# A Fourier mixing layer and two expert layers on one core: conversion steps, first tiles and one weight load in another order

## The chip, the cores and the metric

The kernel runs on one core of a Trainium2 chip, all in 32-bit floats. The time is the device time of one execution in microseconds (us). The engines are TensorE (PE, with its weight loads as PEld), VectorE (DVE), ScalarE (ACT), GpSimd (POOL) and SyncE (SP), which here issues nearly all transfers. Each engine runs its own instructions strictly in the order in which the program gives them; they meet through semaphores.

## The reference

```python
def _attn_ref(x, w_r, w_i, b_r, b_i):            # x: 2 x 3008 x 256
    X = np.fft.rfft(x, axis=1)
    Xr, Xi = (X.real.astype(np.float32), X.imag.astype(np.float32))
    Yr = Xr @ w_r - Xi @ w_i + b_r
    Yi = Xr @ w_i + Xi @ w_r + b_i
    lam = 0.01
    Yr = np.sign(Yr) * np.maximum(np.abs(Yr) - lam, 0.0)
    Yi = np.sign(Yi) * np.maximum(np.abs(Yi) - lam, 0.0)
    Y = Yr.astype(np.float64) + 1j * Yi.astype(np.float64)
    return np.fft.irfft(Y, n=x.shape[1], axis=1).astype(np.float32)

def _moe_ref(x, w_in, w_out):                    # 6016 x 256, hidden 2048
    h = x @ w_in
    return (h * np.clip(h + 3.0, 0.0, 6.0) / 6.0) @ w_out

def _moe2_ref(x, w_gate, w_val, w_out):          # hidden 1536
    g = x @ w_gate
    return (g * (1.0 / (1.0 + np.exp(-g))) * (x @ w_val)) @ w_out
```

The three run one after the other; the weights of the two expert layers come as 64-bit floats.

## The kernel before

The Fourier transform over 3008 = 47 x 64 points is done in two stages of small matrices. Stage one of batch 0 takes x in 16 tiles (`halves1(i)`): 8 matmuls of all 128 rows and 64 columns, two side by side in the array, and one copy into `zm`, by ScalarE for even tiles and VectorE for odd. Stage one of batch 1 takes 8 double tiles T0 to T7 (`quarters1(i)`): 32 matmuls of 64 rows and 64 columns, four side by side, into two PSUM banks, each copied by one engine, first 64 columns to `ze`, then the rest to `zm`.

Stage two goes by 12 quads p = 0 to 11 (6 of each batch): S(p) (`s2`) multiplies 8 blocks of `zm` or, for the first quad of batch 1, of `ze`, with a table `m`; ScalarE and VectorE evict it as X in a high and a low part, then in the same way the sum (`evict`, whose last part runs one work item later). ln(p,0) and ln(p,1) multiply X with the linear weights `linh`, `linl` (three matrices: real, imaginary and mixed sums), after a first matmul that puts the bias tile `shift` into PSUM; then k, yb, yc and yp take the threshold. A(p) (`ia`) is the first stage back, from yp of both halves and a table `n`; its result goes to DRAM. `post` does the second stage back for a pair of token blocks into `xa`.

All matmuls with weights run in three passes of a high and a low part. The expert weights come as 64-bit words in pieces of 256 a row and are put together by `Convert`: a call of `conv1.step()` moves a pipeline by one piece, with a load on SP (piece i+3), two operations of ScalarE (lines 174, 195) and four of VectorE (lines 199, 179, 192, 183). 32 pieces take 38 steps; the first three only load.

A unit (`unit()`) is one of 32 parts of the first expert layer on the first two token blocks: it makes its conversion steps, splits the previous unit's result (`lower`), projects with six matmuls into `ph`, gates, and accumulates the unit before the previous one with six matmuls into `acc`. Units n = 0 to 16 run inside the quads from p = 8 on, the rest in a loop behind.

The order is written by hand in the list `seq` of work items, one list for all engines; what an item leaves for later (`later`, `due`) is put behind the next item. `amid` holds the steps that prepare the linear weights and the bias; `halves1(i)` takes them out after its copy. The lines behind it:

```python
        if 0 < ORDER.index((b, Q)) < FROM:        # in ln; FROM = 8
            conv1.step()
```

```python
        for _ in range(2 - n % 2):                # in unit
            if not conv1.done():
                conv1.step()
```

PSUM has 8 banks, which the items take in turn until p = 7; from there the items take five in turn and `acc` has three. Behind all this, 903 of the 1133 us are the quads of the two expert layers, in which nothing is changed.

Of the kernel before, what the change touches and what calls it, by code (L numbers as in the profile page):

```python
# [81 lines left out]
def fourier_moe_kernel(ctx: ExitStack, tc: tile.TileContext, x, lin, bias, w1, w2, fwd1, inv2, fwd2,  # L82
# [176 lines left out]
    def prepare():  # L259
        lin_st = ring4("lin_st").rearrange("p (k a b) -> p k a b", k=2, a=2)  # L260
        b_st = spread("b_st")
        load_x(0, 1, every=some)
        nc.sync.dma_start(lin_st, lin)
        load_x(0, 2, every=some)
        for c in (slice(0, 2 * TC), slice(2 * TC, RC)):
# [21 lines left out]
        def shifts(i):  # L287
# [7 lines left out]
        amid.update({  # L295
            7: [lambda: mixed(ALU.subtract)], 8: [lambda: hi(2, 0)], 9: [lambda: mixed(ALU.add)],
            10: [lambda: hi(0, 2), lambda: lo(2, 0)], 11: [lambda: hi(1, 3)], 12: [lambda: lo(0, 2)],
            13: [lambda: lo(1, 3)], 14: [lambda: shifts(0)], 15: [lambda: shifts(1)]})

# [8 lines left out]
    def z(b, Q):  # L308
        return zm[:, Q - b] if Q >= b else ze

    def halves1(i):
        src = room[0, i // 4][:, i % 4 * TC : (i % 4 + 1) * TC]
        p = psf[0]([128, 512], f"p1_{i}")
        for n in range(ND):
            for c in range(2):
                at = 128 * n + 64 * c
                nc.tensor.matmul(p[64 * c : 64 * c + 64, n : n + ND * (2 * GC - 1) + 1 : ND], src[:, at : at + 64],
                                 fwd1_sb[:, : 2 * GC], start=True, stop=True, tile_position=(0, 64 * c))
        copy = (nc.scalar.copy, nc.vector.tensor_copy)[i % 2]
        to = zm.rearrange("p q g (r d) -> p (q g) r d", r=2)[:, :, :, ND * i : ND * (i + 1)]  # L320
        copy(to, p[:, : 2 * ND * GC].rearrange("p (a r n) -> p a r n", r=2, n=ND))
        for g in amid.pop(i, ()):
            g()

    def quarters1(i):
        src = room[1, i // 2][:, i % 2 * 2 * TC : (i % 2 + 1) * 2 * TC]
        p = [psf[0]([128, 512], f"p1_{i}_{r}") for r in range(2)]
        N = 2 * ND
# [6 lines left out]
        for r, copy in enumerate((nc.scalar.copy, nc.vector.tensor_copy)):  # L335
            c = slice(64 * r + N * i, 64 * r + N * (i + 1))
            q = p[r][:, : N * GC].rearrange("p (a n) -> p a n", n=N)
            copy(ze[:, :, c], q[:, :8])
            copy(zm[:, : NQ - 1, :, c].rearrange("p q g n -> p (q g) n"), q[:, 8:])

# [54 lines left out]
    def ln(b, Q, h):  # L395

        if (b, Q) not in n_t:
            n_t[b, Q] = table("n", inv1, Q, 4, f"n{b}_{Q}")
        if 0 < ORDER.index((b, Q)) < FROM:
            conv1.step()  # L400
# [63 lines left out]

    T = [[lambda i=i: quarters1(i)] for i in range(NT // 2)]

# [7 lines left out]

    seq = [prepare] + [lambda i=i: halves1(i) for i in range(NT)] + S(0) + [lambda: load_next(0)] + S(1)
    seq += [lambda: load_next(1)]
    for p in range(len(ORDER)):
        l, a, s = L(p), A(p - 1), S(p + 1) if p else []
        u = [lambda: unit()] if p >= FROM else []
        if p == FROM:  # L480
            seq += l[:1] + s + a + [lambda: post(0, 0), lambda: post(0, 1)] + u + l[1:] + u + u + u
        elif p == NQ + 1:
            seq += l[:1] + s + [lambda: load_first()] + a + l[1:]
        elif p == NQ - 3:
            seq += l[:1] + s + T[0] + a + T[1] + l[1:] + T[2]
        elif p == NQ - 2:
            seq += l[:1] + T[3] + s + T[4] + a + T[5] + l[1:] + T[6]
        elif p == NQ - 1:
            seq += l[:1] + T[7] + a + s + l[1:]
        else:  # L490
            seq += l[:1] + u + s + a + u + l[1:] + u + u
# [133 lines left out]
    def unit():  # L625
# [3 lines left out]

        for _ in range(2 - n % 2):  # L630
            if not conv1.done():
                conv1.step()
        if 0 <= n - 1 < len(units):
# [590 lines left out]
```

## Time and profile before

| what | value |
|---|---|
| median of 3 runs | 1134.98 us (1133.74 to 1135.16) |
| the profiled execution, time | 1134.5 us |
| the profiled execution, span | 1132.7 us |
| TensorE busy | 1117.3 us, 99% of the span |
| VectorE busy | 910.4 us, 80% |
| ScalarE busy | 776.8 us, 69% |
| granted clock of TensorE over the span | 0.999 |

The span runs from the first to the last instruction; 1.8 us of the execution lie around it. In a timeline row stand start and duration in us, engine, line, operation, the tile written and those read, the shape, a count where rows are merged, and in brackets the engine's idle time before and what ended it. A row of windows by stage holds the stretch, its length, the busy time of TensorE, its weight loads, VectorE, ScalarE and GpSimd with instruction counts, then the granted clock of TensorE (1.00 is 2.4 GHz, 0.50 is 1.2), the busy share of the transfers and GB/s. Matmuls overlap: the time of a block is the distance of two starts, and a wait is longer than its idle time shows by the part that the previous matmul covers.

### The profile page before, as it was taken

How to read it: one execution, taken by the hardware profiler on the slowest of the kernel's cores; microseconds unless marked ns; L12 is line 12 of the kernel's file. 1: busy time of each engine (PE TensorE's matmuls, PEld its weight loads, DVE VectorE, ACT ScalarE, POOL GpSimd, SP SyncE). 2: the span in 40 equal slices, each digit the busy share in tenths (PEclk: the TensorE clock that was granted, in tenths of full speed). 3: DMA queues.
4: the chain of work that ended last, by engine and by line, in shares of the span. 5: the costliest groups of instructions: out<-in, count | busy, mean ns of one | idle time of the engine just before them, and what ended most of it. 6: DMA issues, size and time to landing. Idle time of an engine off the chain costs nothing.

```text
span 1132.7 us, 19794 instructions
## 1 busy us (share of the span) xinstructions
PE 1117.3 (99%) x7468; PEld 989.2 (87%) x7468; DVE 910.4 (80%) x1635; ACT 776.8 (69%) x1440; POOL 41.4 (4%) x68
## 2 busy tenths in 40 slices
PE   8999999999999999999999999999999999999998
PEld 7988788888888888888899888888888888888997
DVE  5778996899999999999988777777777777777665
ACT  4667775688788788787787666666666666656655
POOL 2000004500000000000000000000000000000000
PEclk9999999999999999999999999999999999999999
DMA  7856434964473664554643544644644644644552
GB/s 288 275 168 191 147 108 144 316 226 171 136 253 109 197 225 154 182 199 149 211 175 127 195 167 167 242 167 168 241 167 168 241 167 168 237 168 168 207 207 75
DMA packets 62944, 211.49 MB, mean 187 GB/s; under 512 B 5984, under 2 KB 23552, under 8 KB 51392
## 3 DMA queue, kind: packets, MB, share of 16 engines
q1 hardware_dynamic: 60784, 203.61, 51.9%
q0 software_dynamic: 1776, 6.42, 1.4%
q8 instruction: 59, 0.97, 0.3%
q14 instruction: 37, 0.30, 0.1%
q10 hardware_dynamic: 288, 0.19, 0.1%
HBM read 170.09 MB, written 40.11 MB: 186 GB/s over the span
## 4 chain that ended last, share of the span: by engine, by line
PE 91%; DVE 5%; DMA 1%; ACT 1%; issue 1%; SPq 0%; ACTq 0%; DVEq 0%
PE acc L133 12%; PE acc L131 12%; PE acc L132 12%; PE P L912 8%; PE P L914 8%; PE P L913 8%; PE Tb L912 4%; PE Tb L913 4%; PE Tb L914 4%; PE Q L912 2%; PE Q L913 2%; PE Q L914 2%; PE p L440 2%; PE p L360 2%; PE p L551 1%
## 5 line engine op out<-in xcount | busy, mean ns | idle before, releaser
L969 ACT COPY hold<-P 128x512 f32<-128x512 f32 (+1 forms) x224 | 128.3, 573 | 57.9 <-PE P L914 56.4
L591 ACT CAST gated<-r 128x512 fp32r<-128x512 f32 (+1 forms) x160 | 98.1, 613 | 64.9 <-DVE r L960 63.3
L136 DVE TENSOR_TENSOR gated<-s,gated 128x512 fp32r<-128x512 f32 (+1 forms) x144 | 97.4, 676 | 49.8 <-ACT gated L1096 49.5
L136 DVE TENSOR_TENSOR gated<-r,gated 128x512 fp32r<-128x512 f32 (+1 forms) x160 | 107.8, 674 | 21.6 <-ACT gated L591 16.9
L131 PE MATMUL acc<-gated,w_o 128*128 128x512 f32 (+1 forms) x320 | 120.4, 376 | 0.0
L132 PE MATMUL acc<-gated,w_o 128*128 128x512 f32 (+1 forms) x320 | 119.6, 374 | 0.0
L133 PE MATMUL acc<-gated,w_o 128*128 128x512 f32 (+1 forms) x320 | 119.6, 374 | 0.0
L964 DVE TENSOR_TENSOR hold<-Q,hold 128x512 f32<-128x512 f32 (+1 forms) x112 | 75.7, 676 | 44.1 <-ACT hold L969 41.8
L133 PE MATMUL acc<-gated,slot 128*128 128x512 f32 (+1 forms) x288 | 108.1, 375 | 0.0
L131 PE MATMUL acc<-gated,slot 128*128 128x512 f32 (+1 forms) x288 | 108.0, 375 | 0.1
L132 PE MATMUL acc<-gated,slot 128*128 128x512 f32 (+1 forms) x288 | 107.9, 375 | 0.0
L964 DVE TENSOR_TENSOR hold<-P,hold 128x512 f32<-128x512 f32 (+1 forms) x112 | 75.7, 676 | 33.9 <-PE P L914 33.9
L1136 ACT ACTIVATE s<-hold 128x512 f32<-128x512 f32 (+1 forms) x72 | 44.9, 623 | 81.0 <-DVE hold L964 81.0
L956 ACT ACTIVATE r<-hold,consts 128x512 f32<-128x512 f32 (+1 forms) x120 | 85.5, 712 | 14.5 <-DVE hold L964 12.4
L912 PE MATMUL P<-xo,slot 128*128 128x512 f32 (+1 forms) x240 | 90.0, 375 | 1.5 <-DVE hold L964 1.4
L1096 ACT CAST gated<-s 128x512 fp32r<-128x512 f32 (+1 forms) x144 | 87.7, 609 | 3.5 <-DVE s L1151 3.3
L913 PE MATMUL P<-xo,slot 128*128 128x512 f32 (+1 forms) x240 | 88.8, 370 | 0.0
L914 PE MATMUL P<-xo,slot 128*128 128x512 f32 (+1 forms) x240 | 88.8, 370 | 0.0
L964 DVE TENSOR_TENSOR hold<-Tb,hold 128x512 f32<-128x512 f32 (+1 forms) x112 | 75.8, 676 | 14.2 <-PE Tb L914 10.5
L960 DVE SCALAR_TENSOR_TENSOR r<-r,hold 128x512 f32<-128x512 f32 (+1 forms) x120 | 80.8, 673 | 2.5 <-ACT r L956 1.4
L1141 ACT ACTIVATE s<-hold 128x512 f32<-128x512 f32 (+1 forms) x72 | 44.8, 622 | 45.7 <-DVE hold L964 45.7
L969 ACT COPY hold<-Tb 128x512 f32<-128x512 f32 (+1 forms) x112 | 65.0, 580 | 4.3 <-ACT hold L969 0.3
(189 smaller groups left out, 2835.0 us busy)
## 6 DMA issues: line engine op xcount, KB each, us to landing
slot<-Wd SPq DMA_DIRECT2D x72, 1152.0 KB
slot<-Sd SPq DMA_DIRECT2D x40, 896.0 KB
st<-in_w SPq DMA_DIRECT2D x68, 256.0 KB
Wd<-slot SPq DMA_DIRECT2D x12, 1152.0 KB
m<-in_fwd SPq DMA_DIRECT2D x12, 512.0 KB
Cd<-cs POOLq DMA_DIRECT2D x12, 512.0 KB, 5.8
Xd<-x SPq DMA_DIRECT2D x20, 256.0 KB
raw<-Xd SPq DMA_DIRECT2D x5, 1024.0 KB
```

The costliest lines, as they stand in the source:

```text
L131: nc.tensor.matmul(o, wl, xh, start=start, stop=False)
L132: nc.tensor.matmul(o, wh, xh, start=False, stop=False)
L133: nc.tensor.matmul(o, wh, xl, start=False, stop=stop)
L136: nc.vector.tensor_tensor(out=o, in0=full, in1=hi.bitcast(F32), op=ALU.subtract)
L591: nc.scalar.copy(hi[:, :n], g[:, :n])
L912: nc.tensor.matmul(o, wl, hi, start=start, stop=False, skip_group_check=not start)
L913: nc.tensor.matmul(o, wh, lo, start=False, stop=False, skip_group_check=not start)
L914: nc.tensor.matmul(o, wh, hi, start=False, stop=True, skip_group_check=not start)
L956: nc.scalar.activation(r[:, :n], x[:, :n], AF.Relu, bias=three)
L964: nc.vector.tensor_tensor(out=h, in0=x[:, :n], in1=c, op=ALU.add)
L969: nc.scalar.copy(c, x[:, :n])
L1096: nc.scalar.copy(hi[:, :nb], t[:, :nb])
```

## The change

Five things are put elsewhere; no arithmetic is changed.

- The linear weights are loaded behind the third of four slices of x, instead of ahead of it.
- Tiles 12 to 15 of batch 0 are made as two double tiles by `quarters1(0, 6)` and `quarters1(0, 7)`, which write only `zm`.
- The steps in `amid` are spread otherwise: four of them (high and low part of the second mixed weight, the two steps of the bias) now run after S(0) and its eviction, ahead of S(1).
- Conversion steps: quad 0 gets two, the double tiles 1, 2, 4, 5, 6, 7 of batch 1 one each, and each unit makes one instead of two and one by turns. The double tiles stand otherwise around A(3), S(5), A(4) and S(6).
- At p = 8, ln(8,1) stands directly behind the two `post` items, and one unit is taken out there; it runs in the loop behind.

```diff
         load_x(0, 1, every=some)
+        load_x(0, 2, every=some)
         nc.sync.dma_start(lin_st, lin)
-        load_x(0, 2, every=some)
...
         amid.update({
-            7: [lambda: mixed(ALU.subtract)], 8: [lambda: hi(2, 0)], 9: [lambda: mixed(ALU.add)],
...
+            14: [lambda: hi(1, 3), lambda: lo(1, 3), lambda: shifts(0), lambda: shifts(1)]})
...
+    def aside(i):
+        for g in amid.pop(i, ()):
+            g()
...
         for r, copy in enumerate((nc.scalar.copy, nc.vector.tensor_copy)):
...
-            copy(ze[:, :, c], q[:, :8])
-            copy(zm[:, : NQ - 1, :, c].rearrange("p q g n -> p (q g) n"), q[:, 8:])
+            if b:
+                copy(ze[:, :, c], q[:, :8])
+            copy(zm[:, : NQ - b, :, c].rearrange("p q g n -> p (q g) n"), q[:, 8 * b :])
+        if b and i not in (0, 3):
+            conv1.step()
+        if not b:
+            aside(NT // 2 - 2 + i)
...
-        if 0 < ORDER.index((b, Q)) < FROM:
+        if ORDER.index((b, Q)) < FROM:
             conv1.step()
...
-    seq = [prepare] + [lambda i=i: halves1(i) for i in range(NT)] + S(0) + [lambda: load_next(0)] + S(1)
+    seq = [prepare] + [lambda i=i: halves1(i) for i in range(NT - 4)]
+    seq += [lambda i=i: quarters1(0, i) for i in (6, 7)] + S(0) + [lambda: load_next(0), lambda: aside(14)] + S(1)
...
         if p == FROM:
-            seq += l[:1] + s + a + [lambda: post(0, 0), lambda: post(0, 1)] + u + l[1:] + u + u + u
+            seq += l[:1] + s + a + [lambda: post(0, 0), lambda: post(0, 1)] + l[1:] + u + u + u
...
         elif p == NQ - 2:
-            seq += l[:1] + T[3] + s + T[4] + a + T[5] + l[1:] + T[6]
+            seq += l[:1] + T[3] + a + T[4] + s + l[1:] + T[5]
         elif p == NQ - 1:
-            seq += l[:1] + T[7] + a + s + l[1:]
+            seq += l[:1] + T[6] + a + T[7] + s + l[1:]
...
-        for _ in range(2 - n % 2):
-            if not conv1.done():
-                conv1.step()
+        if not conv1.done():
+            conv1.step()
```

VectorE around S(0), before: `sum` and `X` with p_0_0 are the eviction of S(0), `linl` and `shift` the last steps of `amid`.

```order
L136 TENSOR_TENSOR linl<-mixed,linh 128x512
L290 TENSOR_SCALAR b_st<-b_st 64x512
L321 COPY zm<-p_15_316 128x96x4
L136 TENSOR_TENSOR shift<-b_st,shift 32x512
L372 TENSOR_TENSOR sum_0_0_348<-p_0_0_0_330,sum_0_0_348 128x256
L136 TENSOR_TENSOR X_0_329<-p_0_0_0_330,X_0_329 128x512
L372 TENSOR_TENSOR sum_0_1_353<-p_0_0_1_331,sum_0_1_353 128x256
```

The same place in the changed program, from the copy of the last double tile to the first of S(1)'s eviction:

```order
L343 COPY zm<-p_0_7_1_318 128x48x8
L136 TENSOR_TENSOR linl<-mixed,linh 128x512
L380 TENSOR_TENSOR sum_0_0_375<-p_0_0_0_357,sum_0_0_375 128x256
L136 TENSOR_TENSOR X_0_356<-p_0_0_0_357,X_0_356 128x512
L380 TENSOR_TENSOR sum_0_1_380<-p_0_0_1_358,sum_0_1_380 128x256
L136 TENSOR_TENSOR X_0_356<-p_0_0_1_358,X_0_356 128x512
L136 TENSOR_TENSOR X_0_356<-sum_0_0_375,X_0_356 128x256
L136 TENSOR_TENSOR X_0_356<-sum_0_1_380,X_0_356 128x256
L136 TENSOR_TENSOR linl<-mixed,linh 128x512
L290 TENSOR_SCALAR b_st<-b_st 64x512
L136 TENSOR_TENSOR shift<-b_st,shift 32x512
L380 TENSOR_TENSOR sum_1_0_417<-p_0_1_0_399,sum_1_0_417 128x256
```

The write of `shift` moved from ahead of S(0)'s eviction to behind the whole of it.

VectorE at the last double tile of batch 1, before: `ze` and `zm` with p_7_1 are T7's copies, `sum` with p_1_0 is S(6).

```order
L423 TENSOR_TENSOR yb_5_0_1255<-p_0_5_0_1232,k_5_0_1253 128x512
L338 COPY ze<-p_7_1_1260 128x8x8
L339 COPY zm<-p_7_1_1260 128x40x8
L429 SCALAR_TENSOR_TENSOR yp_5_0_1258<-yb_5_0_1255,yc_5_0_1257 128x512
L372 TENSOR_TENSOR sum_0_0_1334<-p_1_0_0_1316,sum_0_0_1334 128x256
```

And in the changed program, where the lines 199, 179, 192 and 183 are one conversion step:

```order
L431 TENSOR_TENSOR yb_5_0_1309<-p_0_5_0_1286,k_5_0_1307 128x512
L342 COPY ze<-p_1_6_1_1314 128x8x8
L343 COPY zm<-p_1_6_1_1314 128x40x8
L199 TENSOR_TENSOR w_o<-wt,w_o 128x256
L179 TENSOR_SCALAR wt<-head 128x256
L192 SCALAR_TENSOR_TENSOR wt<-head,wt 128x256
L183 SCALAR_TENSOR_TENSOR wt<-st,wt 128x256
L437 SCALAR_TENSOR_TENSOR yp_5_0_1312<-yb_5_0_1309,yc_5_0_1311 128x512
L342 COPY ze<-p_1_7_1_1379 128x8x8
L343 COPY zm<-p_1_7_1_1379 128x40x8
L199 TENSOR_TENSOR w_g<-wt,w_g 128x256
```

T7's copies moved behind T6's copies, a conversion step and yp, with the eviction of S(6) next but for one more step.

VectorE behind `post`, before: `xa` is the last low part of `post`, `r` with `ph` the gate of the first unit, `yb` that of ln(8,1).

```order
L136 TENSOR_TENSOR xa<-p_0_1_1_1784,xa 128x512
L199 TENSOR_TENSOR w_c<-wt,w_c 128x256
L179 TENSOR_SCALAR wt<-head 128x256
L192 SCALAR_TENSOR_TENSOR wt<-head,wt 128x256
L183 SCALAR_TENSOR_TENSOR wt<-st,wt 128x256
L199 TENSOR_TENSOR w_o<-wt,w_o 128x256
L179 TENSOR_SCALAR wt<-head 128x256
L192 SCALAR_TENSOR_TENSOR wt<-head,wt 128x256
L183 SCALAR_TENSOR_TENSOR wt<-st,wt 128x256
L576 SCALAR_TENSOR_TENSOR r<-r,ph 128x512
L423 TENSOR_TENSOR yb_2_1_1887<-p_1_2_1_1864,k_2_1_1885 128x512
```

And in the changed program:

```order
L136 TENSOR_TENSOR xa<-p_0_1_1_1897,xa 128x512
L431 TENSOR_TENSOR yb_2_1_1969<-p_1_2_1_1946,k_2_1_1967 128x512
L199 TENSOR_TENSOR w_g<-wt,w_g 128x256
L179 TENSOR_SCALAR wt<-head 128x256
L192 SCALAR_TENSOR_TENSOR wt<-head,wt 128x256
L183 SCALAR_TENSOR_TENSOR wt<-st,wt 128x256
L437 SCALAR_TENSOR_TENSOR yp_2_1_1972<-yb_2_1_1969,yc_2_1_1971 128x512
L585 SCALAR_TENSOR_TENSOR r<-r,ph 128x512
```

One of the two steps ahead of the first gate is gone, and ln(8,1) stands ahead of it.

## Rows read from the trace of the kernel before

**Rows 1.** Page, parts 1 and 3: engines' busy time, instruction queue

```profile
PE 1117.3 (99%) x7468; PEld 989.2 (87%) x7468; DVE 910.4 (80%) x1635; ACT 776.8 (69%) x1440; POOL 41.4 (4%) x68
...
q8 instruction: 59, 0.97, 0.3%
```

**Rows 2.** Windows by stage: 47.1 to 77 and 109 to 123 us

```profile
47.10:77.00 29.90, 28.81 (x706) 26.18 (x707) 21.82 (x54) 18.67 (x51) 1.06 (x2) 1.00 0.49 165
...
109.00:123.00 14.00, 11.86 (x86) 9.23 (x79) 13.51 (x34) 10.08 (x24) 0.00 (x0) 1.00 0.45 138
```

**Rows 3.** Timeline of TensorE, first 30 us

```profile
13.06 5.50 PE L317 MATMUL p<-fwd_sb,first 128*64 128x96 f32 x128 [1.11 <-DMA first<-in_x]
19.33 3.84 PE L360 MATMUL p<-m,zm 64*128 64x128 f32 x64 [0.77 <-issue]
23.10 0.48 PE L415 MATMUL p<-shift,ones 128*128 128x512 f32 x1
...
25.84 0.38 PE L415 MATMUL p<-shift,ones 128*128 128x512 f32 x1
...
28.06 0.38 PE L415 MATMUL p<-shift,ones 128*128 128x512 f32 x1
```

**Rows 4.** Timeline of GpSimd, VectorE and ScalarE around the first S

```profile
11.22 2.49 POOL L279 TENSOR_TENSOR mixed<-lin_st 128x512 f32<-128x512 f32 x2 [4.52 <-DMA lin_st<-in_lin]
...
18.35 0.41 DVE L290 TENSOR_SCALAR b_st<-b_st 64x512 f32<-64x512 f32 x1
...
18.80 0.62 ACT L291 CAST shift<-b_st 64x512 fp32r<-64x512 f32 x1 [0.38 <-DVE b_st L290]
...
19.45 0.68 DVE L136 TENSOR_TENSOR shift<-b_st,shift 32x512 fp32r<-32x512 f32 x1 [0.22 <-ACT shift L291]
21.39 0.37 ACT L370 COPY sum<-p 128x256 f32<-128x256 f32 x1 [1.97 <-PE p L360]
...
24.15 0.75 DVE L136 TENSOR_TENSOR X<-sum,X 128x256 fp32r<-128x256 f32 x2
```

**Rows 5.** Timeline of TensorE at tiles T2, T3 and T6

```profile
55.59 1.15 PE L333 MATMUL p<-fwd_sb,second 64*64 64x48 f32 x64
...
60.10 0.62 PE L333 MATMUL p<-fwd_sb,second 64*64 64x48 f32 x27 [0.46 <-issue]
...
74.58 0.43 PE L333 MATMUL p<-fwd_sb,room 64*64 64x48 f32 x10 [0.63 <-issue]
74.94 2.00 PE L440 MATMUL p<-yp,n 64*128 64x256 f32 x16
```

**Rows 6.** Timeline of VectorE in quads 4 and 5

```profile
57.98 0.69 DVE L429 SCALAR_TENSOR_TENSOR yp<-yb,yc 128x512 f32<-128x512 f32 x1 [0.53 <-ACT yc L428]
58.59 0.42 DVE L199 TENSOR_TENSOR w_c<-wt,w_c 128x256 fp32r<-128x256 f32 x1
...
59.80 0.68 DVE L423 TENSOR_TENSOR yb<-p,k 128x512 f32<-128x512 f32 x1
...
63.91 0.42 DVE L372 TENSOR_TENSOR sum<-p,sum 128x256 f32<-128x256 f32 x1 [0.98 <-ACT X L371]
...
65.78 0.21 DVE L338 COPY ze<-p 128x64 f32<-128x64 f32 x1
...
66.31 0.75 DVE L136 TENSOR_TENSOR X<-sum,X 128x256 fp32r<-128x256 f32 x2
```

**Rows 7.** Timeline of TensorE at the first units

```profile
116.98 0.48 PE L133 MATMUL acc<-gs,w_o 128*128 128x512 f32 x1 [0.44 <-DVE gs L136]
...
120.91 0.48 PE L131 MATMUL acc<-gs,w_o 128*128 128x512 f32 x1 [1.50 <-ACT gs L591]
...
121.78 0.48 PE L133 MATMUL acc<-gs,w_o 128*128 128x512 f32 x1 [0.17 <-DVE gs L136]
```

**Rows 8.** Windows by stage: the end of the span

```profile
1129.00:1131.00 2.00, 0.00 (x0) 0.00 (x0) 0.39 (x1) 0.34 (x1) 0.00 (x0) 1.00 0.95 350
1131.00:1132.70 1.70, 0.00 (x0) 0.00 (x0) 0.00 (x0) 0.00 (x0) 0.00 (x0) 0.59 0.07 23
```

More of the change, by code (lines that the diff above doesn't have):

```diff
@@ L295, in prepare @@
         amid.update({
-            7: [lambda: mixed(ALU.subtract)], 8: [lambda: hi(2, 0)], 9: [lambda: mixed(ALU.add)],
-            10: [lambda: hi(0, 2), lambda: lo(2, 0)], 11: [lambda: hi(1, 3)], 12: [lambda: lo(0, 2)],
-            13: [lambda: lo(1, 3)], 14: [lambda: shifts(0)], 15: [lambda: shifts(1)]})
+            7: [lambda: mixed(ALU.subtract), lambda: mixed(ALU.add)], 10: [lambda: hi(2, 0)], 11: [lambda: lo(2, 0)],
+            12: [lambda: hi(0, 2)], 13: [lambda: lo(0, 2)],
+            14: [lambda: hi(1, 3), lambda: lo(1, 3), lambda: shifts(0), lambda: shifts(1)]})
     amid = {}
@@ L321, in halves1, with quarters1 @@
         copy(to, p[:, : 2 * ND * GC].rearrange("p (a r n) -> p a r n", r=2, n=ND))
[L322 to L327, printed above, removed]
+        aside(i)
+    def quarters1(b, i):
+        src = room[b, i // 2][:, i % 2 * 2 * TC : (i % 2 + 1) * 2 * TC]
+        p = [psf[0]([128, 512], f"p1_{b}_{i}_{r}") for r in range(2)]
         N = 2 * ND
@@ L463, in A @@
         return [lambda: ia(*ORDER[p])] if p >= 0 else []
-    T = [[lambda i=i: quarters1(i)] for i in range(NT // 2)]
+    T = [[lambda i=i: quarters1(1, i)] for i in range(NT // 2)]
     def load_next(k):
```

## The prediction

> **What bounds the kernel now.** I read the page's busy shares first: TensorE is busy 99% of the span [rows 1]. Since matmuls overlap, that hides waits, so I went by starts of consecutive blocks of TensorE. In the windows by stage the only place where TensorE is visibly short of work is 109 to 123 us (11.86 busy of 14), where VectorE is at 13.51 of 14; in 47.1 to 77 VectorE is busy 21.82 of 29.9 [rows 2]. From 226 us to the end nothing is touched by the change, and I give it no difference. So a gain can only come from three places: the start, the quads with the second batch's tiles, and the first units. I call the eight-matrix stage of quad p S(p), its two linear halves ln(p,0) and ln(p,1), the inverse A(p), the second batch's tiles T0 to T7.
>
> **1. The start.** Before, the tiles of the third x slice begin at 13.06 us after 1.11 us of waiting for x; eight of them take 5.50 us; S(0) starts at 19.33 and the first ln at 23.10, that is 3.77 us after S(0) with no wait between [rows 3]. The linear weights land just before 11.22 us, when GpSimd starts on them [rows 4], ahead of that x slice. Exchanged, x comes about 1.8 us earlier (13.06 less 11.22), so the wait of 1.11 us goes and tiles 8 to 11 end near 14.6. Two quarter tiles of 1.1 us each [rows 5] take the place of four tiles of 5.50/8 = 0.69 us: 2.2 for 2.8. The second of them waits for the last x piece, whose place is unchanged; I put its end at 16.8 and S(0), after one copy, at 17.6: 1.7 us earlier than 19.33.
>
> Both engines run in order, and in the new order four steps that stood between tile copies stand behind S(0)'s eviction and ahead of S(1)'s: the cast and rest of the second mixed weight, and the two steps of the bias. The first ln's first matmul reads the bias tile. The chain from S(0)'s start: ScalarE's first copy at +2.06 (19.33 to 21.39); X and sums of one dh pair out by VectorE until its last pair of operations starts at +2.76 more (21.39 to 24.15) and is issued in about 0.7 (of 0.75); the rest of the weight 0.60 (an operation of 0.68, pipelined); bias addition to ScalarE's cast 0.45 (18.35 to 18.80), cast to VectorE's rest 0.65 (18.80 to 19.45), that rest 0.68 [rows 4]. Sum 7.9 us, so the first ln starts at 17.6 + 7.9 = 25.5, where TensorE is done with S(1) at 17.6 + 3.8 = 21.4. It idles 4.1 us. Before, that ln took 2.74 us (23.10 to 25.84) with a wait of 0.5 inside against 2.22 for the next (25.84 to 28.06) [rows 3]; that 0.5 goes, because X is long there. End of ln(0,0): 25.84 before, 25.5 + 2.2 = 27.75 after. **Cost +1.9 us** (bounds +1.2, if x and copies come 0.7 sooner, and +2.8, if the second quarter tile starts late).
>
> A rule that speaks against the quarters: the Trainium skill, TensorEngine Tiling, section PSUM Bottleneck, says that tiling speeds TensorE but not the copies out of PSUM, which can then bind. By it the 0.6 us saved on the four tiles would be lost; by the rows a quarter tile's ze and zm copies follow one another in 0.53 us on VectorE, half a tile's time, so I let the saving stand. It matters little, since the bias chain ends later either way.
>
> **2. The granted clock.** It is 1.00 up to 1131 us, and 0.59 in the last stretch: after TensorE had issued nothing from 1129 us on, the clock went from the upper (2.4 GHz) to the lower level (1.2) within about 2 us [rows 8]. A gap of 4.1 us at the start is longer than that. I take it that the clock falls there, and that the matmuls after the gap run at half pace for a while. No row of before shows this inside the kernel. Bounds: 0, and the doubling of one whole ln, 2.2 us [rows 3]. **Value +1.2**, half of that, since part of the low stretch falls into the gap itself.
>
> The Trainium skill, TensorE: Matmul & The Clock Gate, section Why this matters for your kernels, wants no idle gaps between bursts of matmuls, because the clock goes back to half. The trace agrees at its end only; without the rule the sum would be 1.2 us lower, which is the first rival.
>
> **3. Conversion steps moved.** One full step costs VectorE 1.21 us (58.59 to 59.80) [rows 6]. The two steps put into quad 0 only issue loads of 256 KB on SP's queue; SP is past x and m by then, the weights are wanted ten steps later, and what stands behind them (a room of x, the n tables) is read more than 5 us after it lands: nothing. Since all steps come two earlier, quads 1 and 2 get a little more work under TensorE: nothing. The six steps behind T1, T2, T4 to T7 add 6 x 1.21 = 7.3 us to VectorE between 47.1 and 77, where it had 8.1 us idle [rows 2]. It is the order that decides. Up to S(5) VectorE still waits for TensorE in my walk. From the end of S(5): 1.0 until its first operation, eviction 1.87 (63.91 to 65.78), step 1.21, last pair 0.7, yb 0.61, T5's copies 0.53 (65.78 to 66.31), step 1.21, yp 0.61 (57.98 to 58.59), step 1.21, yb 0.61, T6's copies 0.53, step 1.21, yp 0.61, then T7's ze copy 0.2 [rows 6]: 12.1 us. TensorE's own work from there to the end of T7 is two ln (2.3 each), three tiles (1.1), A(4) (1.9, of 2.00): 9.8 us [rows 3, 5]. S(6) now stands right behind T7 and reads ze, which T7's copies write; before, A(4) stood between. So **S(6) waits about 2.3 us** (bounds: 0.4, the bare latency of a copy, and see the slower rival).
>
> **4. T tiles in another order.** Before, T3 and T6 stop in the middle, at 60.10 and 74.58, with idle time of 0.46 and 0.63 us that ended by "issue", nothing else [rows 5]; counted from starts, the two tiles took 0.7 and 0.9 us too long. The queue of kind instruction moves 0.97 MB in 59 packets [rows 1] for 14,936 TensorE records, 65 bytes each, so 253 records a packet: a quarter tile of 64 matmuls and 64 weight loads uses half a packet in 1.1 us. I read these stops as TensorE outrunning its code. The new start has 128 records more, so the packet borders move by half a packet, and T4, T5, T6 and T7 stand between slower blocks. Gain 1.6, less 0.3 for a border that may now fall into T2 or the first quarters: **-1.3** (bounds -1.6 and 0).
>
> **5. Units.** Before, TensorE stops at 116.98, 120.91 and 121.78 for the high and low parts of the first units (idle 0.44, 1.50, 0.17, each about 0.17 more from start to start) [rows 7]; 2.6 us. Waits that pipelining hides whole (each of these shows 0.17 less than it costs) I estimate at 1.0 more over the sixteen units that convert; sum 3.6. Cause: two steps (2.4 us of VectorE) in every other unit of 2.6 us. After, ln(8,1) stands ahead of the first unit, so that the post copies drain, and each unit has one step. Walk of the first unit: yb 0.6, step 1.2, yp 0.6, r 0.6, step 1.2, low part 0.7 from yb's start at about 112.1 gives 117.0; the accumulation wants it at 115.9: 1.1 to 1.2 us of waiting left once, then none. **-2.4** (bounds -1.5 and -3.6). The unit taken out of the quads returns in the loop behind, at the same 2.6 us.
>
> **Sum.** +1.9 + 1.2 + 2.3 - 1.3 - 2.4 = +1.7 us on the profiled execution's 1134.5, 1136.2. The median of the runs shown is 0.5 above it; on the median the forecast is 1136.6.
>
> **Rivals.** Clock holds (0.2): the gap is there, the clock is not taken; 1135.4. For it: no fall at 12 us, where TensorE waited 1.1 us; against: the fall after the last matmul.
> Quarters fit (0.15): VectorE and ScalarE overlap better than my walk, S(6) waits 0.4; 1134.7. For it: the walk takes whole spacings; against: 7.3 us into 8.1 idle leaves little.
> VectorE is full from T2 on (0.15), the slower side: the idle that VectorE has at turnarounds (1.0 at each eviction, 0.5 at each yc) cannot be filled, some 5 us in that stretch; then 21.8 + 7.3 + 5 = 34.1 us for 29.9, up to 4.2 longer than before instead of 1.0. It decides if VectorE is already busy when S(5) ends. At 3 us more than the forecast: 1139.6.
> More gained (0.08): units gain 3.6, S(6) waits 0.4, the clock holds: 1.6 - 1.2 - 1.9 - 1.2 = -2.7 from the median: 1132.3.
> Forecast as summed: 0.42, its own range 1135.2 to 1138.0.
>
> **How the numbers follow.** 0.2% is 2.27 us, about what a measurement can tell here: 1132.7 and 1137.3. Slower: the slower rival 0.15, a third of the forecast's case 0.14, 0.01 of the rest: 0.30. Faster: the last rival 0.08 and 0.03 of clock holds and quarters fit: 0.11. Same: 0.59. The range, 1132.8 to 1139.2, leaves out the far ends of the slower and the faster rival.
>
> **What would show it.** In the profile after: a wait of TensorE of about 4 us on VectorE's shift tile at the first ln, near 21.4 to 25.5; granted clock under 1.00 in the windows behind it; a wait at S(6)'s first matmul on the ze copy; no "issue" idle in the quarter tiles; one wait of about 1 us at the first accumulation, none at the second. Wrong if the first ln starts by 23 us, or if S(6) follows T7 within 0.5 us, or if the unit waits remain.

## The result, and the profile after

| | kernel before | changed kernel |
|---|---|---|
| median of the executions (lowest to highest), us | 1134.15 (1133.57 to 1135.16), six | 1143.41 (1141.37 to 1146.93), six |
| profiled execution, and its span, us | 1134.50, 1132.7 | 1141.91, 1140.1 |
| mean granted clock of the profiled execution | 1.00 up to 1131 us | 0.995 |

The change makes the kernel slower by 9.3 us: ratio 1.0083, interval 1.0065 to 1.0101. The forecast was 1136.6, its range ended at 1139.2. The changed kernel also spreads over 5.6 us where the one before spread over 1.6; its six executions have mean clocks of 0.995, 0.995, 0.994, 0.992, 0.992 and 0.992, in the order of their times.

Starts of TensorE's blocks in the two profiled executions, in us, show where the time went:

| start of | before | after | later by |
|---|---|---|---|
| S(0) | 19.33 | 18.43 | -0.90 |
| ln(0,1) | 25.84 | 31.94 | 6.10 |
| T0 | 49.09 | 55.33 | 6.24 |
| S(6) | 76.77 | 83.56 | 6.79 |
| ln(5,1), behind S(6) | 78.65 | 87.08 | 8.43 |
| `post` | 105.97 | 114.39 | 8.42 |
| end of `post` | 109.35 | 119.80 | 10.45 |
| first block of the loop behind the units | 225.57 | 233.67 | 8.10 |
| end of the span | 1132.70 | 1140.13 | 7.43 |

Three places lose (6.1, 1.6 and 2.0 us), the units give 2.35 back. The first, in the timeline of TensorE after (start, busy time, instruction, idle before it and what ended that), with the last step on `shift` from that of VectorE:

```profile
9.94 5.50 PE L321 MATMUL p<-fwd_sb,first 128*64 128x96 f32 x128 [2.03 <-DMA first<-in_x]
...
18.43 1.57 PE L368 MATMUL p<-m,zm 64*128 64x128 f32 x22 [0.74 <-ACT zm L343]
20.84 2.61 PE L368 MATMUL p<-m,zm 64*128 64x128 f32 x42 [0.84 <-issue]
27.54 0.77 PE L423 MATMUL p<-shift,ones 128*128 128x512 f32 x1 [4.09 <-DVE shift L136]
...
31.94 0.51 PE L423 MATMUL p<-shift,ones 128*128 128x512 f32 x1
...
26.72 0.68 DVE L136 TENSOR_TENSOR shift<-b_st,shift 32x512 fp32r<-32x512 f32 x1 [0.68 <-ACT shift L291]
```

These answer to [rows 3]. The wait on `shift` is there, 4.09 us. Inside S(0) stands a stop named issue, for which the view finds no releaser, and which the kernel before didn't have, and from 27.54 to 31.94 one ln takes 4.40 us, where 2.74 was before. Windows by stage after (width, busy time of each engine, granted clock, share of the DMA engines, GB/s) tell why:

```profile
23.18:27.44 4.26, 0.28 (x5) 0.08 (x1) 3.53 (x8) 2.63 (x8) 0.00 (x0) 0.76 0.82 293
27.44:31.94 4.50, 4.40 (x19) 4.34 (x20) 2.62 (x6) 1.45 (x4) 0.00 (x0) 0.50 0.98 320
...
55.33:81.40 26.07, 26.07 (x670) 23.49 (x668) 23.64 (x66) 20.56 (x57) 1.06 (x2) 1.00 0.55 185
81.40:83.56 2.16, 0.07 (x8) 0.04 (x1) 2.16 (x8) 2.16 (x7) 0.53 (x1) 0.96 0.92 286
83.56:87.08 3.52, 3.52 (x33) 3.40 (x33) 1.50 (x5) 0.21 (x1) 0.00 (x0) 0.54 0.98 331
...
114.39:119.80 5.41, 3.32 (x178) 3.06 (x177) 3.56 (x7) 2.94 (x7) 0.53 (x1) 1.00 0.78 307
```

The clock is at its lower level through ln(0,0), from 25.4 to 32.2 us by its records. It falls again behind the 2.16 us between T7 and S(6), from 83.4 to 86.8: S(6) takes 3.52 us instead of 1.88. That wait is the one forecast, as the timeline of VectorE after shows, with one row of ScalarE's behind it; it answers to [rows 6]:

```profile
80.91 0.21 DVE L342 COPY ze<-p 128x64 f32<-128x64 f32 x1
81.04 0.47 DVE L343 COPY zm<-p 128x320 f32<-128x320 f32 x1
81.44 0.41 DVE L199 TENSOR_TENSOR w_o<-wt,w_o 128x256 fp32r<-128x256 f32 x1
...
82.64 0.68 DVE L437 SCALAR_TENSOR_TENSOR yp<-yb,yc 128x512 f32<-128x512 f32 x1
83.24 0.21 DVE L342 COPY ze<-p 128x64 f32<-128x64 f32 x1
...
82.59 0.22 ACT L342 COPY ze<-p 128x64 f32<-128x64 f32 x1
```

T7's last matmul starts at 81.25, but its `ze` copy stands behind T6's copies, one conversion step and yp, and starts at 83.24; S(6) at 83.56. VectorE has no idle time there. The view names ScalarE's w_o as what ended S(6)'s wait; the order of VectorE and the times name `ze`: ScalarE's half of it was copied 0.65 us earlier, and S(6) starts 0.1 us behind the end of VectorE's.

The third loss is inside `post`, again in the timeline of TensorE after:

```profile
114.39 0.31 PE L560 MATMUL p<-inv_sb,ct 48*64 48x47 f32 x2
115.07 2.07 PE L560 MATMUL p<-inv_sb,ct 48*64 48x47 f32 x124 [0.37 <-ACT X L379]
118.86 1.01 PE L560 MATMUL p<-inv_sb,ct 48*64 48x47 f32 x50 [1.72 <-issue]
```

No operand is missing at 116.9 to 118.9, and `post` takes 5.41 us instead of 3.38. In the DMA view of 116.1 to 116.5 us of the same execution (queue and kind: packets, MB, share) a block of code starts to arrive:

```profile
q8 instruction: 1, 0.02, 18.9%
```

The units, TensorE's timeline after, for [rows 7]: two waits left at the first accumulation, none at the second.

```profile
126.57 0.48 PE L131 MATMUL acc<-gs,w_o 128*128 128x512 f32 x1 [0.39 <-ACT gs L600]
...
127.79 0.48 PE L133 MATMUL acc<-gs,w_o 128*128 128x512 f32 x1 [0.52 <-DVE gs L136]
```

### The profile page after: what moved, and what is told of

It reads as the page before. It is cut to its first block, busy times and chain, and to the rows that moved or that the text cites. A ratio compares the mean times of both kernels' runs of the same rounds, so it can differ in the third digit from the quotient of the medians.

```text
span 1140.1 us, 19913 instructions
## 1 busy us (share of the span) xinstructions
PE 1118.7 (98%) x7532; PEld 994.2 (87%) x7532; DVE 909.6 (80%) x1635; ACT 776.8 (68%) x1440; POOL 41.6 (4%) x68
## 4 chain that ended last, share of the span: by engine, by line
PE 90%; DVE 6%; ACT 2%; issue 1%; DMA 1%; POOL 0%; SPq 0%; DVEq 0%; ACTq 0%; POOLq 0%
PE acc L131 12%; PE acc L133 12%; PE acc L132 12%; PE P L920 8%; PE P L922 8%; PE P L921 8%; PE Tb L921 4%; PE Tb L922 4%; PE Tb L920 4%; PE Q L922 2%; PE Q L921 2%; PE Q L920 2%; PE p L368 2%; PE p L448 2%; PE p L560 1%
## 5 line engine op out<-in xcount | busy, mean ns | idle before, releaser
L136 DVE TENSOR_TENSOR gated<-r,gated 128x512 fp32r<-128x512 f32 (+1 forms) x160 | 107.9, 674 | 21.4 <-ACT gated L600 16.9
L1144 ACT ACTIVATE s<-hold 128x512 f32<-128x512 f32 (+1 forms) x72 | 44.9, 623 | 81.4 <-DVE hold L972 81.4
```

What stands on the lines that cost most here:

```text
L136: nc.vector.tensor_tensor(out=o, in0=full, in1=hi.bitcast(F32), op=ALU.subtract)
```

## The experiments

Theory: the 9 us are four separate things, the wait on `shift`, the clock behind it, VectorE's backlog at S(6) with a second fall of the clock, and stops for code in S(0) and `post`. Rival: the clock falls because of the dense quarter tiles, and the stop belongs to `post` as such. Times are medians, each beside the kernel before on the same chip (1134.68 us for e1 to e4); the changed kernel's 1143.41 stands beside 1134.15. A ratio goes by all times of a run and can lean the other way than the medians. Edits of e5 to e10 are given in short, partly in words.

**e1, the steps on `shift` ahead of S(0).**

```
-  12: [hi(0, 2)], 13: [lo(0, 2)],
-  14: [hi(1, 3), lo(1, 3), shifts(0), shifts(1)]
+  12: [hi(0, 2)],
+  13: [lo(0, 2), shifts(0), hi(1, 3), shifts(1), lo(1, 3)]
```

> The changed kernel with one edit: the steps on `shift` and the last mixed weight (hi(1,3), lo(1,3), shifts(0), shifts(1)) stand behind the last quarter tile, ahead of S(0), instead of behind S(0). Theory (the wait on `shift` at the first ln makes the gap, and the gap makes the clock fall): ln(0,0) starts at about 23.3 us in place of 27.5, granted clock 1.00 through it, ln(0,1) starts at about 25.9 in place of 31.9, T0 at about 49 in place of 55.3; the time falls by about 6.1 us, to some 1137.3. Rival (the clock falls for another cause, the denser quarter tiles): the gap goes and the half-speed stretch of 6.8 us stays; the time falls by about 4.1 us, to 1139.3. The wait at S(6) (2.1 us) and the stop in `post` (1.7 us) stay in both.

1137.55 us (1133.94 to 1139.46), before 1134.68. Windows of the profiled execution, around S(0), around T7's end and S(6):

```profile
17.80:23.00 5.20, 4.09 (x64) 3.78 (x64) 3.07 (x6) 2.92 (x7) 0.00 (x0) 1.00 0.31 87
...
74.90:77.10 2.20, 0.17 (x12) 0.04 (x4) 2.20 (x8) 2.20 (x7) 0.52 (x1) 1.00 0.90 289
77.15:79.14 1.99, 1.99 (x33) 1.87 (x33) 1.50 (x5) 0.22 (x1) 0.00 (x0) 1.00 0.98 299
```

The gap and the slow stretch are gone together: ln(0,0) starts at 23.00, ln(0,1) at 25.66, T0 at 48.92. The edit gives 5.9 us of 9.3 on the medians, where the theory said 6.1; that they agree so well is in part luck, for the profiled execution without the slow stretch is at 1133.94. S(6) still waits 2.08 us, here without a fall of the clock: that this wait takes the clock is not the rule. The two stops for code stay, 1.11 us idle in S(0) and 1.48 in `post`, here in TensorE's timeline:

```profile
20.46 2.61 PE L368 MATMUL p<-m,zm 64*128 64x128 f32 x42 [1.11 <-issue]
...
110.61 1.01 PE L560 MATMUL p<-inv_sb,ct 48*64 48x47 f32 x51 [1.48 <-issue]
```

This profile is of the fastest of ten executions; the seven with a mean clock of 0.997 or less took 1136.65 to 1139.46, and where their clock fell is not known.

**e2, the gap filled.**

```
+  if (b, Q, h) == (0, 0, 0):
+      for _ in range(2):
+          nc.tensor.matmul(p.rearrange("r c d -> r (c d)"), zm[:, 0, 0], zm[:, 0, :4].rearrange("p g c -> p (g c)"),
+                           start=True, stop=True)
```

> The changed kernel with the gap ahead of ln(0,0) filled: two float32 products of 512 columns (about 1.7 us each) on the first quad's transformed input, into the bank that ln(0,0) then overwrites; no result changes. `shift` is as late as before. Theory (idle time of TensorE makes the clock fall): ln(0,0) starts at 27.5 as in the changed kernel, but at clock 1.00, and takes about 2.4 us instead of 4.4; the time falls by about 2.2 us to 1141.2. Rival (the clock falls for another cause): the stretch at 0.50 stays, time 1143 or a little more.

1142.65 us. The two products have 512 columns each. In the profile ln(0,0) ran at full clock and took 2.30 us, so with work in the gap the clock was up for it; but the clock fell in two other places:

```profile
28.03:30.33 2.30, 2.30 (x19) 2.27 (x20) 2.30 (x6) 1.35 (x4) 0.00 (x0) 1.00 0.96 308
113.50:116.94 3.44, 0.23 (x16) 0.10 (x7) 1.29 (x2) 0.86 (x2) 0.00 (x0) 0.68 0.61 239
116.94:121.60 4.66, 4.66 (x67) 4.49 (x68) 1.29 (x2) 1.07 (x2) 0.00 (x0) 0.50 0.01 4
```

The stop in `post` was 3.2 us idle this time and took the clock with it; so did the stop in S(0), 1.93 us idle, with a low stretch from 22.6 to 26.0, over before ln(0,0). What the filled gap gave went there. The time alone would have spoken for the rival; the rows don't.

**e3, two steps less behind T tiles.**

```
-  if b and i not in (0, 3): conv1.step()
+  if b and i not in (0, 3, 5, 6): conv1.step()
   def ia(b, Q):
+      if (b, Q) in (ORDER[5], ORDER[6]): conv1.step()
```

> The changed kernel with two of the six conversion steps that stand behind T tiles (those of T5 and T6) moved behind A(5) and A(6), where VectorE has idle time. Theory (VectorE's backlog of 1.36 us a step holds back T7's copy to `ze`, S(6) waits for that, and the wait makes the clock fall again): the 2.1 us wait ahead of S(6) falls under 0.6, S(6) takes 1.9 us instead of 3.5 at clock 1.00, and the time falls by 3 to 3.7 us, to about 1140. Rival (the wait and the second clock fall are separate): the wait goes, S(6) stays at 3.5 us, the time falls by about 2 us, to 1141.4. A third outcome: the two steps cost as much in quads 7 and 8 and the time does not move.

1140.74 us. TensorE's timeline, S(6) and the S behind ln(8,0):

```profile
82.71 1.50 PE L368 MATMUL p<-m,ze 64*128 64x128 f32 x22 [0.54 <-ACT ze L342]
...
110.23 2.11 PE L368 MATMUL p<-m,zm 64*128 64x128 f32 x26 [1.55 <-DVE yb L431]
```

The wait at S(6) fell to 0.54 and the clock held: VectorE's backlog is its cause. In exchange the steps of A(6) and ln(7,1), which stand one behind the other in VectorE's queue, held up a yb, and S(9) waited 1.55 us for its bank. In this profile the clock fell there.

**e4, other code borders.**

```
-  for n in (512, 320):
+  for n in (320,) + (16,) * 24:
       nc.tensor.matmul(p[:, :n], zeros[:, :128], zeros[:, :n], start=True, stop=True)
```

> The changed kernel with other warm-up matmuls at its very start, ahead of the first input's arrival: one of 320 columns and 24 of 16 columns in place of one of 512 and one of 320, so that some 92 more instruction records stand ahead of everything else on TensorE. Theory (the stops named issue are TensorE running out of loaded instructions where many short matmuls stand in a row, and where it happens depends on where the blocks of loaded code end): the stop of 1.7 us in `post` at 117 moves or shrinks, and so does that of 0.8 us in S(0); post takes about 3.4 us if it holds none; the time falls by up to 2 us to 1141.4, unless the stop appears in another row of short matmuls. Rival (post's stop belongs to post, whatever lies ahead of it): it stays at 1.7 us in the same place, and the time is 1143.4.

1145.21 us. The short products cost far more than I had reckoned, their 48 matmul records come every 0.21 us and the x tiles start at 12.94 instead of 4.99, so the time says little. But the stops did move:

```profile
25.37 3.84 PE L368 MATMUL p<-m,zm 64*128 64x128 f32 x64 [0.74 <-ACT zm L343]
...
120.29 1.62 PE L560 MATMUL p<-inv_sb,ct 48*64 48x42 f32 x96 [0.44 <-issue]
```

S(0) has none, `post` has 0.44 us idle instead of 1.72 and takes 4.04 us. The stop stands behind its 80th matmul instead of its 126th, and 46 matmuls is what the edit added ahead of it: its place is set by the count of instructions from the program's start, and not by `post`. Of the 7.95 us lost at the start, 5.8 are left at ln(0,0), 3.4 at `post` and 2.0 behind it.

**e5 and e6, the two halves of the change.** e5 takes back the start:

```
   load_x(0, 1, every=some)
-  load_x(0, 2, every=some)
   nc.sync.dma_start(lin_st, lin)
+  load_x(0, 2, every=some)
-  halves1(0..11), quarters1(0, 6), quarters1(0, 7), S(0), ..., aside(14), S(1)
+  halves1(0..15), S(0), ..., S(1)      (steps behind tiles 7 to 15, as before)
```

> The changed kernel with the start of the kernel before: second x slice after `lin`, all sixteen half tiles, the mixed-weight and `shift` steps behind half tiles 7 to 15; everything from S(0) on as changed. Theory (the start costs 6.1 us by T0, and its 60 or so additional instructions on TensorE put the end of a block of code into `post`, for another 2 us): T0 at 49.1 us as before; no stop in S(0); post takes about 3.4 us as before; the wait ahead of S(6) stays at 2.1 us. Time 1143.4 - 6.2 - 2.0 = 1135.2, or some 1.5 us more in executions where the clock falls at S(6). Rival (post's stop comes from what stands around it now, ln instead of a unit): post stays at 5.1 to 5.4 us and the time is about 1137.2. By the prediction's steps the rest alone is worth 2.3 - 1.3 - 2.4 = -1.4, so 1132.8 if nothing else were added.

e6 keeps the start and takes back all the rest:

```
-  if ORDER.index((b, Q)) < FROM: conv1.step()
+  if 0 < ORDER.index((b, Q)) < FROM: conv1.step()
-  if b and i not in (0, 3): conv1.step()
-  post, post, l[1:], u, u, u
+  post, post, u, l[1:], u, u, u
-  l[:1], T3, A, T4, S, l[1:], T5  |  l[:1], T6, A, T7, S, l[1:]
+  l[:1], T3, S, T4, A, T5, l[1:], T6  |  l[:1], T7, A, S, l[1:]
-  one step a unit
+  two steps in every other unit
```

> The changed kernel with everything after S(1) as in the kernel before (no steps behind T tiles nor in quad 0, before's order of T tiles, post and first unit, two steps in every second unit): the start alone is changed. Theory: ln(0,0) starts at 27.4 us with the clock at 0.50 behind it, T0 about 6.2 us later than before; S(6) has no wait (VectorE has no steps of T tiles); the time is 1134.3 + 6.2 = 1140.5, and up to 2 us more where the shifted code blocks end in `post` or in T tiles. Rival (the start is absorbed by later waits, for example by the units' waits for converted weights): under 1138.

e5: 1134.83 us, before 1134.86, ratio 1.0001 (0.9992 to 1.0009). e6: 1141.26, ratio 1.0065 (1.0048 to 1.0082). The start carries most of the loss, the rest by itself is worth nothing. The profiled execution of e6, 1145.45, is the slowest of its four (the others 1140.17 to 1141.56), and its clock fell in three places, at 26.1, 114.9 and 131.9 us. TensorE's timeline of e5, S(0), S(6) and `post`, and the row in `post` of e6:

```profile
20.23 3.84 PE L368 MATMUL p<-m,zm 64*128 64x128 f32 x64 [0.77 <-issue]
...
78.22 1.01 PE L368 MATMUL p<-m,ze 64*128 64x128 f32 x13 [2.08 <-ACT w_o L195]
...
108.18 2.77 PE L560 MATMUL p<-inv_sb,ct 48*64 48x47 f32 x174 [0.37 <-ACT X L379]
```

```profile
116.09 1.72 PE L558 MATMUL p<-inv_sb,ct 48*64 48x47 f32 x52 [2.26 <-issue]
```

S(0) is whole again (the 0.77 ahead of it is there before too [rows 3]; it ends with the copy of the last x tile, see e9). `post` without the changed start has no stop, though ln stands behind it as in the changed kernel (the 0.37 is a wait inside it that the kernel before has too); with the changed start it stops, though a unit stands behind it. So the stop comes from what lies ahead of `post` in the code, 64 matmuls more, and not from its neighbours. S(6)'s wait is in e5 and belongs to the steps.

**e7, e8 and e10, other places for the steps**, all with the start of before. e7 moves the steps of T5 and T6 behind A(5) and into the first unit:

```
-  if b and i not in (0, 3): conv1.step()
+  if b and i not in (0, 3, 5, 6): conv1.step()
   in ia:    + if (b, Q) == ORDER[5]: conv1.step()
   in unit:  - one step    + two steps if n == 0, else one
```

> e5 (start of the kernel before, rest as changed) with two conversion steps fewer behind T tiles: those of T5 and T6 go behind A(5) and into the first unit. Theory (VectorE's backlog makes the wait at S(6)): that wait falls from 2.1 us to under 0.8, with it the clock's falls at S(6); the first unit pays at most 0.7 us for its second step. Time about 1.5 to 2 us under that of e5, some 1133, which is 1 us under the kernel before. Rival (as with e3, the moved steps cost elsewhere what they give): the same as e5.

1134.49 us (before 1134.86; 1.0002, 0.9992 to 1.0011). The wait moved from S(6), 0.38 idle, to the first accumulation, where the clock fell too (119.1 to 122.5); and T7 has a stop for code, in TensorE's timeline:

```profile
74.93 0.60 PE L336 MATMUL p<-fwd_sb,room 64*64 64x48 f32 x25 [0.47 <-issue]
75.92 2.06 PE L368 MATMUL p<-m,ze 64*128 64x128 f32 x32 [0.38 <-ACT ze L342]
...
117.66 0.48 PE L131 MATMUL acc<-gs,w_o 128*128 128x512 f32 x1 [1.66 <-ACT gs L602]
```

e8 moves three steps forward:

```
-  if b and i not in (0, 3): conv1.step()
+  if b and i in (1, 2, 7): conv1.step()
   in ia:    + if (b, Q) in ORDER[:3]: conv1.step()
```

> e5 (start of the kernel before, rest as changed) with three of the six steps behind T tiles (T4, T5, T6) moved forward, behind A(0), A(1) and A(2), where VectorE has idle time. Theory: VectorE has no backlog at T7, the 2.1 us wait at S(6) falls under 0.4, and since no step goes behind S(6) nothing comes back at the units; time about 2 us under e5's 1134.8, near 1132.8. Rival (the early steps' 262 KB loads press on the input transfers, which fill the DMA engines at 26 to 42 us): the wait goes from S(6) to T0 or to a table in quads 2 and 3, and the time stays at 1134.8.

1134.37 us (before 1134.52; 0.9996, 0.9986 to 1.0006). S(6) waits 0.55, but ln(3,0) takes 3.21 us instead of 2.32 and A(3) waits 1.05 for a yp of VectorE. e10 takes all six off the T tiles, in the order of T tiles of before, and issues five early:

```
   behind S(1), quad 0, quad 1:   + conv1.step()
   in ia:    + if (b, Q) in ORDER[:2]: conv1.step()
   (no step behind T tiles; ln of quad 0, post and units as changed)
```

> The kernel before (its start, its order of T tiles, S and A) with the change's units only: one conversion step a unit, the second ln of quad 8 right behind post, a step in each ln of quad 0, and, in place of the six steps behind T tiles, four early ones: behind S(1), behind quads 0 and 1, and behind A(0) and A(1) (five with both). Theory (the units' part is worth 2.4 us; early steps cost nothing where VectorE has idle time; with no step behind T tiles there is no wait at S(6)): time 1134.5 - 2.4 = 1132.1, faster than both kernels. Rival (the early weight loads press on the input transfers that fill the DMA engines at 26 to 42 us, and T0 or a table comes later): 1133.5 to 1135.

1136.99 us (before 1135.4; 1.0018, 1.0007 to 1.0028): slower. TensorE loses over 5 us between 36 and 52 us, ln(3,0) alone takes 6.19, waiting for operands from ScalarE and VectorE:

```profile
47.14 0.38 PE L418 MATMUL p<-linl,X 128*128 128x256 f32 x1 [0.75 <-ACT X L379]
48.20 0.38 PE L420 MATMUL p<-linh,X 128*128 128x256 f32 x1 [0.57 <-DVE X L136]
```

VectorE has steps ahead of each eviction and yb there, two in a row from 42.5 to 44.9 us. Behind the first waits the clock fell as well, from 49.1 to 52.5, which makes about 1.5 of the 5 us. The rival said the DMA engines; the rows say VectorE's queue and the clock behind it.

**e9, e1 with half tiles.**

```
-  halves1(0..11), quarters1(0, 6), quarters1(0, 7)
+  halves1(0..15)      (steps as in e1, behind tiles 7 and 10 to 13)
```

> e1 (changed kernel, steps on `shift` ahead of S(0)) with half tiles 12 to 15 in place of the two quarter tiles; `lin` stays behind the second x slice. This asks what the quarter tiles themselves cost or give. Theory (256 dense instruction records ahead of S(0) make TensorE run out of loaded code in S(0), and the additional records put a block's end into `post`): no stop in S(0), post back at 3.4 us, S(0) starts about 0.9 us later than with quarters; the time is 1137.5 - 1.4 - 1.7 + 0.9 = 1135.3. Rival (the quarter tiles shorten the start, the stops lie elsewhere): 1138.4.

1135.07 us (before 1134.52; 1.0001, 0.9989 to 1.0013), 2.5 under e1, nearly as expected. `post` took 3.38 us, without a stop for code:

```profile
109.91 2.77 PE L560 MATMUL p<-inv_sb,ct 48*64 48x47 f32 x174 [0.37 <-ACT X L379]
```

That the time agrees is in part luck, for S(0) came at 20.73, 2 us later than expected, behind 2.86 us idle that took the clock too (21.4 to 24.8). Its row says issue; but VectorE's timeline has the last tile's copy behind a step that was now ahead of it, and S(0) starts 0.1 us behind the end of that copy. In the kernel before it is the same, with the copy in the third row and S(0) at 19.33:

```profile
19.46 0.69 DVE L136 TENSOR_TENSOR linl<-mixed,linh 128x512 fp32r<-128x512 f32 x1
20.07 0.55 DVE L325 COPY zm<-p 128x384 f32<-128x384 f32 x1
...
18.68 0.54 DVE L321 COPY zm<-p 128x384 f32<-128x384 f32 x1
```

So issue is what is left where the view finds no releaser, and not every such row is code.

**g12 and g21, a gap made in the kernel before.**

```
   in ln, ahead of its first matmul, for (b, Q, h) == (0, 2, 0):
+      nc.gpsimd.tensor_copy(inv2_sb, X[b, Q][1][:, 0, 2, :96].bitcast(F32))
+      for _ in range(12):      (g21: 21)
+          nc.gpsimd.tensor_copy(inv2_sb, inv2_sb)
+      nc.tensor.matmul(p[:96, 0, :96], inv2_sb, inv2_sb, start=True, stop=True)
```

> The kernel before with one made gap: the first ln of quad 2 waits for a chain of 13 small copies on GpSimd (idle there), through one small product into the bank that ln then overwrites. It asks what a wait of about 2 us costs TensorE. Theory (a wait of this size costs itself, and in some executions a stretch at half clock behind it): gap 1.5 to 2.5 us, time 1134.5 plus the gap, with a spread upward of 1.5 us or more among the runs. Rival (the clock falls only behind longer waits): the gap alone, with the spread of the kernel before.

> The same with 22 copies: a wait of about 4 us. Theory: granted clock 0.50 for 3.4 to 7 us right behind the gap in every execution, 1.5 to 3 us lost beside the gap: time 1134.5 + 4 + 2.3 = 1141. Rival (what fell at the first ln of the changed kernel was not due to the gap): 1138.5.

1142.79 and 1146.01 us, before 1134.52. A copy took 0.36 us, more than I had taken, and the gaps came out at 5.5 and 8.5 us from start to start. So no row here prices a made gap of 2 us. Windows behind the gap of g12, and of g21:

```profile
42.50:47.30 4.80, 4.80 (x21) 4.57 (x21) 0.00 (x0) 0.00 (x0) 0.00 (x0) 0.50 0.07 26
```

```profile
44.55:50.07 5.52, 5.52 (x27) 5.20 (x29) 0.12 (x1) 0.37 (x1) 0.00 (x0) 0.50 0.01 3
```

The clock fell in both and stayed low for 4.8 and 5.5 us of work behind the gap. At half pace that loses 2.4 and 2.8 us; with the gaps, 7.9 and 11.3, where 8.3 and 11.5 were measured. In the changed kernel it was 4.7 us of work (27.5 to 32.2), so 2.3 us. This differs from one execution to the next: behind the same wait on `shift` it was 5.5 us in e6 and 2.9 in e4.

## Why the prediction was wrong

Two of its steps failed: the border of 0.3 us in step 4, and the size and the single place of the clock's fall in step 2. Every sign that the prediction named came, the wait on `shift` 2 us later than it said; but none of the signs looked at `post` or at a second fall of the clock.

1. **Start, +1.9 forecast.** The wait on `shift` was forecast at 4.1 us and is 4.09; e1 shows that it is the order of the steps. S(0) was put at 17.6 and came at 18.43, because x still kept TensorE 2.03 us; in e1 and e2, with the same loads, S(0) came at 17.8, so this differs from one execution to the next. What the walk left out is the stop inside S(0), 0.84 us idle and 1.1 from start to start: from S(0)'s start to that of ln(0,0) it is 9.1 us instead of 7.9, and the links behind the stop are as forecast to 0.1. T0 is 6.2 us later, where this term and the next said 3.1: 0.8 from x, 1.1 from the stop, 0.1 from the chain, 1.1 from the clock.
2. **Clock, +1.2.** Right in kind: it fell 2.2 us into the gap (3.0 to 3.9 in e4, e6, g12 and g21). Mis-sized, and so one of the two steps that failed: the gap takes 2.3 us, the forecast's upper bound and a little more, since the stretch at half pace went on 4.7 us behind the gap instead of ending in the first ln. And the step looked at one gap only: the clock fell behind S(6)'s wait too, 1.6 us more. The Trainium skill, TensorE: Matmul & The Clock Gate, section Why this matters for your kernels, warns of idle gaps between bursts; g12 and g21 bear it out inside the kernel, with 4.8 and 5.5 us of work at half clock behind the gap.
3. **Steps behind T tiles, +2.3.** Right: 2.08 us of idle at S(6), 2.3 from start to start, and e3 and e7 show the cause. The slower rival, VectorE full from T2 on, did not come: from T0 to T7's end VectorE is 23.64 busy of 26.07, and TensorE waits for nothing until S(6).
4. **T tiles, -1.3.** This is the step whose failure cost most. The stops of [rows 5] did go, from T0 to S(6) the changed kernel loses only 0.55 us, wait included, where this term and the third said 1.0. That they went is owed to where the borders came to lie and not to the new neighbours: the second stop was in T7 (72.92 to 74.94), not in T6, both T3 and T7 stood between longer blocks before as well, and in e7 T7 stops again in the new order. The failure is the last clause, 0.3 us for a border that may now fall elsewhere. It fell into S(0) and `post`, for 1.1 and 2.0 us, 3.1 in all. Having read the stops as TensorE outrunning its code, and reckoned that the borders move by half a packet, I never walked the borders along to the next dense rows; `post`, 176 small matmuls, is the densest there is, and was not in the sum because the change does not touch it. Counting records would have led there, see the last section.
5. **Units, -2.4.** Right: from `post`'s end to the loop 116.22 us before, 113.87 after, 2.35 less; 113.76 and 113.77 in e8 and e9.

In sum, on the profiled executions: 3.1 us more than forecast by T0, 0.45 less from T0 to S(6), 1.6 more at S(6), 2.0 more in `post`, and 0.7 given back in the loop behind, which the forecast put at nothing; 5.6 in all, which with the forecast's 1.7 makes 7.3 of the 7.4 by which the span grew. Four of the other five executions of the changed kernel have a lower mean clock than the profiled one, which would put the median 1.5 us above it; their rows are not there to show it. The forecast's median of 1136.6 is 1136.7 by its own terms, which changes nothing.

Single edits lead back almost all the way: 1143.41 as changed, 1137.55 with the steps on `shift` ahead (e1), 1135.07 with half tiles too (e9), 1134.83 with the loads and steps of before (e5), and 1134.2 to 1135.4 for the kernel before on the chips of these runs. None of the versions beat it clear of the noise.

**Left open.** e5 should be 1.8 us faster than the kernel before by its T stage (+0.55) and units (-2.35), and is level. In its profile, 1.1 us over its median, S(0) came 0.9 us later, the units gave only 0.8, where ScalarE waited 2.48 us for a spill buffer near 215 us, and the loop behind took 0.7 more; e8 and e9 show the whole gain of the units, and losses ahead of it. Whether the other executions of e5 lose it in that way is not known. Also, e6 costs 6.4 us and e5 nothing, but both together 9.3; the second fall of the clock, which only the whole change showed at S(6), would be 1.6 of the 2.9 between, and the rest has no row.

## What to carry to other kernels

When a change adds or removes many short instructions, count TensorE's records on to every dense row further on, touched or not, see which block borders fall into one, and reckon with a stop of up to 3 us there. Price a gap of TensorE at the start of a kernel as the gap plus the half-speed stretch behind it (here 4.1 us cost 6.4), and look for the last link of the chain before moving a small step, such as a bias, behind a large eviction. Where the engine that gets a moved step is busy eight tenths of the time, expect the wait to move with it.

## What the hardware did that was not expected

Code blocks. In twelve stops of TensorE in these profiles (two of the kernel before, two each of the changed kernel, e1, e2, e3 and e6), a 16 KB packet of the instruction queue starts to arrive, and TensorE issues again 2.24 to 2.65 us after that start: 57.85 to 60.10 and 72.28 to 74.58 in the kernel before, 18.42 to 20.84 and 116.21 to 118.86 in the changed one, 114.48 to 116.94 in e2. In nine of them TensorE had gone on for 0.4 to 1.6 us after the packet's start, in three it had started its last matmul 0.1 to 1.0 us before. Five smaller stops, of 0.29 to 0.66 us idle in e4, e7, g21 (two) and e10, go the same way. In `post` a matmul and its weight load go by every 15 ns (124 in 1.9 us), so what was left did not last. Among longer matmuls such a stop shows once: 0.66 us in e10, in the ln behind `post`. The Trainium skill, Runtime: NRT & Kernel Launch, section Instruction fetch mechanics, has code come in blocks of 16 KiB and calls the cost of crossing a border mostly hidden; the size agrees with 0.97 MB in 59 packets here, the cost does not where the row is dense: up to 3.2 us idle in e2.

Where these stops stand is fixed. If one counts TensorE's matmuls, weight loads and semaphore instructions in each trace from the program's start, exactly 705, 1473, 1729, 2497 or 3521 of them come ahead of each of the seventeen stops: the first number and 3, 4, 7 and 11 times 256 more. Number 3521 falls into `post` with the changed start, and into the ln behind `post` with that of before. The waits ahead of S(0) in the kernel before and in e9 stand at 532, at no such border. A border is a place for a stop and not yet a stop: number 3265 lies in `post` before and costs nothing there, and g12 has neither of the stops that g21 has with the same matmuls. What makes a packet come late is not shown.

The clock behind short waits. Behind the gaps of 4.1 to 8.3 us idle it fell each time: in the changed kernel, e4, e6, g12 and g21. Behind the 2.08 us at S(6) it fell in one of six profiles with the same wait (the changed kernel; not e1, e2, e4, e5, e9). Of all eighteen waits of 1.4 to 2.9 us idle from S(0) to the units in these profiles, met at the upper level, the clock fell behind eight, among them 1.66 us at the first accumulation of e7, 1.51 at one of e6, and 1.93 in S(0) of e2; behind 1.50 and 1.51 at an accumulation in the kernel before, g12 and g21 it did not fall. A wait of this size is a chance of a further 1.6 us or more, which makes the spread of the times wider than the waits themselves.
